# Query sketches on eight 32x64 PE tiles, squares over 2048 columns, first loads reordered, all engines replanned

## The chip, the cores and the metric

The kernel runs on one core of one Trainium2 chip. Its engines are PE (TensorE, matmuls; PEld is its weight load), DVE (VectorE), ACT (ScalarE), POOL (GpSimd) and SP (SyncE, which here only issues DMAs). The metric is device microseconds of one launch, as the median of several runs. Matmuls write PSUM, which has eight banks of 512 float32 per partition; a name such as L447 is line 447 of the kernel before.

## The reference, cut to what matters

```python
# q, k, v: (4 batches, 4 heads, 1088 tokens, 32); S1, S2: (8, 32), all float32
def phi(x):                                   # 32 -> 64 features
    a = einsum('rd,bhsd->bhsr', S1, x)
    b = einsum('rd,bhsd->bhsr', S2, x)
    return einsum('bhsi,bhsj->bhsij', a, b).reshape(..., 64)
q_p, k_p = phi(q), phi(k)
kv  = einsum('bhsf,bhsd->bhfd', k_p, v);  z = k_p.sum(axis=2)
num = einsum('bhsf,bhfd->bhsd', q_p, kv)
den = einsum('bhsf,bhf->bhs', q_p, z)[..., None] + 1e-06
x = (num / den)  as (4352 tokens, 128)        # heads side by side
h = x @ w_in;  g = maximum(h, 0) ** 2         # w_in: 128 x 2048
out = g @ w_out                               # w_out: 2048 x 128
```

## The kernel before, in words

There are two parts, interleaved on all engines: a linear attention, batch by batch (`attention(b, vt)`), and a feed-forward over blocks of tokens (`ffn`).

**Attention of one batch.** SP loads k, q and v (L297, L333, L340), with four heads times 32 rows of tokens on the 128 partitions, and 34 tokens of 32 numbers side by side. DVE transposes k and q in 32x32 blocks (`tk` L365, `tq` L434), so that heads times 32 dimensions are on the partitions. For k, PE multiplies 32-column slices with the block-diagonal sketch `SK` (`ksk` L379), ACT copies one half of the result (`ka` L387), DVE multiplies both halves to 64 features (`kp` L395), and PE accumulates `kv` and `z` over all tokens (`kv` L412) in the one PSUM bank `a`; two small copies bring it to `kvz` (`kve` L425).

**The query sketch** stands at L440 to L464. A batch's 1088 query columns are handled in three groups of 384, 384 and 320. For each of S1 and S2 (`x`), PE runs two matmuls of 64 rows by 128 columns, one for each pair of heads (`qr` L447); `SR` holds a sketch repeated so that the product has all 64 features of both heads. Each fp32 matmul shows as two records in the profile. S1's result lies in one two-bank PSUM buffer `hA`, S2's in another, `hB`. ACT copies `hA` to SBUF (`qa` L456), which frees `hA`, and DVE multiplies `hB` with that copy into `qp` (`qp` L460), which frees `hB`.

Then PE forms numerator and denominator (`num` L477, 24 matmuls of 128x32 for a group), DVE divides (`mx`, L487 to L489), PE transposes (`tx` L500) and ACT or DVE writes the token columns into `xT` (`xe` L506).

**Feed-forward.** Nine blocks of 384, 7x512 and 384 tokens; 2048 hidden columns make eight pairs of 128 for each block. For a pair, PE makes two matmuls into an `h` buffer (`m1` L527), ACT applies Relu to bf16 (`r` L536), DVE squares 128x1024 (`g` L543), and PE accumulates two matmuls into `o` (`m2` L550). At the end of a block DVE transposes `o` (`oe` L557) and SP stores it (`st` L566) in pieces of 32 output dimensions. Weights come through POOL's queue, cast to bf16 (L275, L279), behind a small POOL copy that waits for the second piece of the first k (`gate` L271).

**PSUM**: three `h` buffers of two banks each, one `o` bank and one `a` bank: all eight. `num`, `tx` and `ksk` take `a` or `h`; sketches and `m1` take only `h`.

**The order** is the work of a small planner in the file (`Graph.run`, L62). Each operation has a cost for each engine that may do it, its predecessors, the buffers it needs and a due time `pri`; among the operations that can start within a look-ahead (`LOOK`) of the earliest one, the one with the least `pri` goes first, and where two engines are possible the one that ends first, with a penalty (0.6 us for a Relu on DVE). The list it gives is the order in which each engine issues. At most eight DMAs of the hardware queues are under way by its rule at L95.

```python
181  NH, NA, NR, NB = 3, 1, 4, 2
539  o2 = add(f"r.{n}.{m}", {"ACT": act(W * N), "DVE": dve(W * N, fix=0.16) + (0.6,)}, ...
544  o3 = add(f"g.{n}.{m}", {"DVE": dve(W * N, 0.53e-3, 0.1)}, ...
```

Of the kernel before, what the change touches and what calls it, by code (L numbers as in the profile page):

```python
# [15 lines left out]
SEM = 0.07  # L16
LOOK = 0.12
DMA_FIRST = 1.05
DMA_LAST = 1.2

# [8 lines left out]
class Op:  # L29
    def __init__(self, name, alts, fn, deps, pri, alloc, uses, port, dma, after):  # L30
        self.name, self.alts, self.fn, self.pri = name, alts, fn, pri
        self.deps = [d for d in deps if d is not None]
        self.alloc, self.uses, self.port, self.dma = alloc, uses, port, dma
        self.after = [d for d in after if d is not None]
        self.look = LOOK
        self.start = self.end = self.eng = None


class Graph:
# [22 lines left out]
    def run(self):  # L62
        eng_free, port_free, pipe = {}, 0.0, 0.0
# [8 lines left out]
        while ready:  # L72
            cands = []
            for o in ready:
# [11 lines left out]
                for e, (busy, lat, *pen) in o.alts.items():  # L86
                    pen = pen[0] if pen else 0.0
# [5 lines left out]
                    if e in o.port:  # L93
                        t = max(t, port_free)
                    if o.dma is not None and e != "POOL" and len(lanes) >= 8:  # L95
                        t = max(t, lanes[-8])
# [16 lines left out]
            eng_free[e] = t + busy  # L113
            if e in o.port:
                port_free = t + busy
# [15 lines left out]
def act(n):  # L131
    return (0.833e-3 * n + 0.17, 0.833e-3 * n + 0.2)


def dve(n, rate=1.042e-3, fix=0.07):
    return (rate * n + fix, rate * n + fix + 0.04)
# [6 lines left out]
def pe(t):  # L143
    return (t, t + 0.2)


@with_exitstack
def kernel(
# [29 lines left out]
    def P(name, shape, dt=F32):  # L178
        return ps.tile(shape, dt, name=name, tag=name)

    NH, NA, NR, NB = 3, 1, 4, 2
    G = Graph({"h": NH, "o": 1, "a": NA, "r": NR, "g": NR, "osb": 3, "den": 3, "A": 2})
    tiles = {
        "h": [P(f"h{i}", [128, 1024]) for i in range(NH)],
        "o": [P("o0", [128, 512])],
        "a": [P(f"a{i}", [128, 512]) for i in range(NA)],
        "r": [T(f"r{i}", [128, 1024], BF16) for i in range(NR)],
        "g": [T(f"g{i}", [128, 1024], BF16) for i in range(NR)],
        "osb": [T(f"osb{i}", [128, 512]) for i in range(3)],
        "den": [(T(f"den{i}", [128, 12]), T(f"rec{i}", [128, 12]), T(f"xs{i}", [128, 3, 128], BF16)) for i in range(3)],  # L190
        "A": [T(f"A{i}", [128, 2, 384]) for i in range(2)],
    }

    def at(buf):
        return tiles[buf.slot[0]][buf.slot[1]]

# [6 lines left out]
    mk2 = T("mk2", [128, 2])  # L203
    SK = T("SK", [128, 2, H, R])
    SR = T("SR", [128, 2, 2, R, R])
# [8 lines left out]
    vtl = [T(f"vtl{i}", [32, H, 2, D]) for i in range(NB)]  # L214
# [3 lines left out]
    kvz = [T(f"kvz{i}", [128, 2, 2, D + 1]) for i in range(NB)]  # L218
    qp = [T(f"qp{i}", [128, 2, S]) for i in range(NB)]
# [3 lines left out]
    SU = [None, None]  # L223
    for x, src in ((0, S1), (1, S2)):
        def f(e, x=x, src=src):
            en = nc.sync if e == "SP" else nc.scalar
            en.dma_start(out=S_sb[x::2, :], in_=src[None, :, :].to_broadcast([8, R, D]))  # L227
        SU[x] = add(f"S{x}", {"SP" if x else "ACT": (0.4, 2.0)}, f, pri=-200, dma=0.05)
    o_mkz = add("mkz", {"DVE": dve(4)}, lambda e: nc.vector.memset(mk4, 0.0), pri=-100)

    def f_mk(e):
        for h in range(H):
            nc.vector.memset(mk4[32 * h : 32 * h + 32, h : h + 1], 1.0)
        nc.vector.tensor_tensor(out=mk2, in0=mk4[:, 0:2], in1=mk4[:, 2:4], op=ALU.add)
    o_mk = add("mk", {"DVE": (0.4, 0.45)}, f_mk, [o_mkz], pri=-100)
    o_ST = add("ST", {"DVE": dve(32)}, lambda e: nc.vector.transpose(ST, S_sb), SU, -98)
# [3 lines left out]
    for x in range(2):  # L240
        def f(e, x=x):
            s = STx[:, x]
            s = s[:, None, None, :] if x else s[:, None, :, None]
            nc.vector.tensor_tensor(
                out=SR[:, x], in0=s.to_broadcast([128, 2, R, R]),
                in1=mk2[:, :, None, None].to_broadcast([128, 2, R, R]), op=ALU.mult)
        o_SR.append(add(f"SR{x}", {"DVE": dve(128)}, f, [o_ST, o_mk], -96))

# [7 lines left out]
    for i in range(NB):  # L256
# [6 lines left out]
        iot, pattern=[[1, 128]], base=0, channel_multiplier=-1), pri=-101)  # L263
# [7 lines left out]
    o_gate = add("gate", {"POOL": (0.1, 0.15)}, lambda e: nc.gpsimd.tensor_copy(gate, kin[0][:, S - 1 : S]), [], -45)  # L271
    gated = [o_gate]
    for lo, hi in ((0, 1), (1, 2), (2, 4)):
        def f(e, lo=lo, hi=hi):
            nc.gpsimd.dma_start(out=w_in[:, 512 * lo : 512 * hi], in_=moe_w_in[:, 512 * lo : 512 * hi])  # L275
        o_win.append(add(f"w_in{lo}", {"POOL": (0.9, 3.0)}, f, [z_ops[1]] + gated, -40 + lo, dma=0.8 * (hi - lo)))
# [3 lines left out]
        o_wout.append(add(f"w_out{lo}", {"POOL": (1.0, 3.0)}, f, [z_ops[1]] + gated, -39.5 + lo, dma=0.9 * (hi - lo)))  # L280
# [5 lines left out]
    hist = {}  # L286

# [3 lines left out]
    def attention(b, vt):  # L291
        i = b % NB
        mine = lambda key, op: hist.setdefault((b, key), []).append(op)

        def ld(dst, src, c0, c1):
            def f(e):
                nc.sync.dma_start(  # L297
                    out=dst[:, D * c0 : D * c1],
                    in_=src[b].rearrange("h (t c) d -> (h t) (c d)", c=C)[:, D * c0 : D * c1])
            return f  # L300

        def tok(j, g):
            if j == 8:
# [6 lines left out]
        o_kh = [add(f"ldk{b}.{c0}", {"SP": (0.4, 3.4)}, ld(kin[i], k, c0, c1), prev(b, "tk"), vt(0) - 30 + c0 / 16,  # L310
                    dma=1.6 * (c1 - c0) / 34) for c0, c1 in KS]
        if b == 0:
            o_gate.deps.append(o_kh[1])
            hist["order"] = []
        after = [] if b == 0 else list(hist["order"])
        if b == 1:
            for o in o_kh:
                o.after += after
        o_q = []
        QS = ((0, 12), (12, 34)) if b == 0 else ((0, 34),)  # L320
        for c0, c1 in QS:
            o_q.append(add(f"ldq{b}.{c0}", {"SP": (0.4, 3.4)}, ld(qin[i], q, c0, c1), prev(b, "tq"),
# [307 lines left out]
```

## Time and profile before

| | us |
|---|---|
| median of 3 runs (132.45 to 136.91) | 133.09 |
| span of the profiled execution | 130.5 |
| PE busy, 1572 matmul records | 115.0 |
| DVE busy, 170 instructions | 96.6 |
| ACT busy, 108 instructions | 81.6 |
| POOL busy, 30 instructions | 11.1 |
| first matmul (`ksk`) starts | 5.59 |
| first `m1` starts | 22.55 |
| last matmul ends, last `oe` starts | 125.5 |

The profiled execution spans 130.5 us from its first instruction to its last, 2.6 us less than the median of the runs; sums below are made against the span, and the 2.6 us are added at the end. Busy time of an engine counts instructions that overlap once. The chain of work that ended last is followed back from the last instruction, at each step to what released it. All DMAs together moved 10.22 MB, nearly all of the input in the first 32 us.

### The profile page before, as it was taken

What the parts mean: (1) busy time and instruction counts of PE and PEld (TensorE: products, weight loads), DVE (VectorE), ACT (ScalarE), POOL (GpSimd) and SP (SyncE); (2) the same over time, 40 slices, a digit from 0 to 9 for tenths busy, and PEclk for the clock granted to TensorE, in tenths of its full rate; (3) what the DMA queues carried; (4) which work ended last, traced back from release to release, by engine and by line L of the source; (5) the groups of instructions that cost most, each with busy time, mean ns of one, the idle gap of its engine ahead of it and who ended that gap; (6) DMA issues with size and microseconds to landing.
All of it is one profiled execution on the core that took longest, in us unless ns stands there. A gap on an engine that the chain in (4) does not pass through costs nothing.

```text
span 130.5 us, 3742 instructions
## 1 busy us (share of the span) xinstructions
PE 115.0 (88%) x1572; PEld 62.2 (48%) x1572; DVE 96.6 (74%) x170; ACT 81.6 (63%) x108; POOL 11.1 (9%) x30
## 2 busy tenths in 40 slices
PE   0279599599999899999999999999999999999930
PEld 0256365353565455455445655556355544444500
DVE  2486367969969999969837888798268977878840
ACT  0065023377636749986525979885377699999910
POOL 4091000504250000000000000000000000000000
PEclk9999959999999999999999999999999999999996
DMA  1999999996700210220130001301300040031402
GB/s 21 296 135 242 328 254 260 254 225 223 159 3 0 51 17 0 40 45 0 28 58 0 5 0 28 57 0 25 60 0 5 0 80 5 3 65 18 78 16 50
DMA packets 24225, 10.22 MB, mean 78 GB/s; under 512 B 19472, under 2 KB 22928, under 8 KB 24208
## 3 DMA queue, kind: packets, MB, share of 16 engines
q1 hardware_dynamic: 22280, 8.57, 28.1%
q0 software_dynamic: 992, 1.05, 5.3%
q10 hardware_dynamic: 936, 0.37, 1.3%
q8 instruction: 12, 0.20, 0.6%
q14 instruction: 5, 0.04, 0.1%
HBM read 8.80 MB, written 2.23 MB: 85 GB/s over the span
## 4 chain that ended last, share of the span: by engine, by line
PE 70%; DMA 9%; DVE 7%; ACT 6%; issue 2%; ACTq 2%; DVEq 0%
PE o L550 21%; PE h L527 18%; PE h L447 14%; ACT r L536 6%; PE a L412 5%; DMA qin<-in_q_dram 5%; PE a L477 4%; DMA vin<-in_v_dram 4%; PE h L477 3%; DVE g L543 3%; PE a L379 2%; DVE osb L557 2%; PE h L500 1%; PE h L379 1%; ACTq L227 1%
## 5 line engine op out<-in xcount | busy, mean ns | idle before, releaser
L536 ACT ACTIVATE r<-h 128x1024 bf16<-128x1024 f32 (+1 forms) x72 | 65.6, 1026 | 19.7 <-PE h L527 19.5
L543 DVE TENSOR_TENSOR g<-r 128x1024 bf16<-128x1024 bf16 (+1 forms) x72 | 46.8, 662 | 11.3 <-ACT r L536 10.7
L550 PE MATMUL o<-g,w_out 128*128 128x512 bf16 (+1 forms) x144 | 40.9, 368 | 0.7 <-DVE g L543 0.4
L527 PE MATMUL h<-xT,w_in 128*128 128x512 bf16 (+1 forms) x144 | 40.1, 369 | 0.7 <-ACT r L536 0.4
L447 PE MATMUL h<-qT,SR 64*128 64x384 f32 (+1 forms) x96 | 22.3, 560 | 1.3 <-DVE qT L434 1.3
L527 PEld LDWEIGHTS <-w_in 128*128 128x128 bf16 x144 | 15.1, 114 | 15.7 <-issue 4.5
L550 PEld LDWEIGHTS <-w_out 128*128 128x128 bf16 x144 | 12.1, 97 | 15.8 <-issue 6.9
L460 DVE TENSOR_TENSOR qp<-h,A 128x768 f32<-128x768 f32 (+1 forms) x12 | 10.9, 907 | 5.7 <-PE h L447 5.1
L456 ACT COPY A<-h 128x768 f32<-128x768 f32 (+1 forms) x12 | 9.2, 763 | 7.5 <-PE h L447 7.5
L447 PEld LDWEIGHTS h<-qT,SR 64*128 64x128 f32 x96 | 8.3, 202 | 9.0 <-issue 4.3
L412 PEld LDWEIGHTS a<-vp,kp 128*64 128x64 f32 x288 | 9.3, 143 | 3.7 <-issue 3.7
L412 PE MATMUL a<-vp,kp 128*64 128x33 f32 x288 | 10.1, 228 | 0.0
L379 PE MATMUL a<-SK,kT 128*32 128x64 f32 x168 | 3.8, 239 | 5.6 <-DVE kT L365 5.6
L365 DVE STREAM_TRANSPOSE kT<-kin 128x1088 f32<-128x1088 f32 (+2 forms) x5 | 5.4, 1073 | 3.0 <-DMA kin<-in_k_dram 3.0
L434 DVE STREAM_TRANSPOSE qT<-qin 128x384 f32<-128x384 f32 (+1 forms) x8 | 5.9, 734 | 2.0 <-DMA qin<-in_q_dram 1.9
L557 DVE STREAM_TRANSPOSE osb<-o 128x512 f32<-128x512 f32 (+1 forms) x9 | 6.1, 682 | 1.0 <-PE o L550 0.8
L395 DVE TENSOR_TENSOR kp<-a,ka 128x1024 f32<-128x1024 f32 (+1 forms) x5 | 6.4, 1272 | 0.6 <-ACT ka L387 0.6
L477 PEld LDWEIGHTS h<-kvz,qp 128*32 128x32 f32 x288 | 5.0, 120 | 3.1 <-issue 1.5
L379 PEld LDWEIGHTS a<-SK,kT 128*32 128x32 f32 x168 | 2.9, 121 | 7.1 <-DVE kT L365 5.6
L350 POOL COPY vp<-vin 128x512 f32<-128x512 f32 x6 | 4.1, 706 | 22.9 <-DMA vin<-in_v_dram 16.2
L477 PE MATMUL h<-kvz,qp 128*32 128x66 f32 x288 | 6.1, 238 | 0.0
L477 PEld LDWEIGHTS a<-kvz,qp 128*32 128x32 f32 x288 | 4.4, 109 | 2.5 <-issue 1.3
(42 smaller groups left out, 55.0 us busy)
## 6 DMA issues: line engine op xcount, KB each, us to landing
kin<-in_k_dram SPq DMA_DIRECT2D x3, 544.0 KB, 8.4
qin<-in_q_dram SPq DMA_DIRECT2D x3, 544.0 KB, 8.2
vin<-in_v_dram SPq DMA_DIRECT2D x12, 128.0 KB, 8.3
out_dram<-osb SPq DMA_DIRECT2D x16, 64.0 KB, 1.9
out_dram<-osb SPq DMA_DIRECT2D x8, 48.0 KB, 2.2
qin<-in_q_dram SPq DMA_DIRECT2D x1, 352.0 KB, 6.6
vin<-in_v_dram ACTq DMA_DIRECT2D x5, 64.0 KB, 4.1
out_dram<-osb SPq DMA_DIRECT2D x8, 40.0 KB, 1.7
```

What stands on the lines that cost most here:

```text
L379: nc.tensor.matmul(o[32 * g : 32 * g + 32, :, j - j0, :], lt, SK.rearrange("p x h r -> p x (h r)"), start=True, stop=True)
L395: nc.vector.tensor_tensor(out=kp[i][:, j0:j1].rearrange("p j h (x y) -> p (j h) x y", y=R), in0=bb[:, :, None, :].to_broadcast([128, m, R, ...
L412: nc.tensor.matmul(t[64 * (h % 2) : 64 * (h % 2) + 64, 33 * (h // 2) : 33 * (h // 2) + 33], kp[i][:, j, h, :], vp[i][:, h, j, :], start=(j ...
L447: nc.tensor.matmul(at(hb)[:, 512 * pr : 512 * pr + n], SR[64 * pr : 64 * pr + 64, x].rearrange("p a x y -> p (a x y)"), qT[i][64 * pr : 64 ...
L456: nc.scalar.copy(at(sA)[:, :, 0:n], at(hA).rearrange("p (m s) -> p m s", m=2)[:, :, 0:n])
L460: nc.vector.tensor_tensor(out=qp[i][:, :, c0 : c0 + n], in0=at(hB).rearrange("p (m s) -> p m s", m=2)[:, :, 0:n], in1=at(sA)[:, :, 0:n], o ...
L477: nc.tensor.matmul(t[32 * cc : 32 * cc + 32, x, 2 * pr : 2 * pr + 2, :], qp[i][:, pr, 32 * c : 32 * c + 32], kvz[i][:, pr], start=True, st ...
L527: nc.tensor.matmul(at(hb)[:, step * w : step * w + N], w_in[:, 512 * (ct // E) : 512 * (ct // E) + 512].rearrange("p (c e) -> p e c", e=E) ...
L536: nc.scalar.activation(o, view(at(hb)), ACTF.Relu)
L543: nc.vector.tensor_tensor(out=at(gb)[:, 0 : W * N], in0=r, in1=r, op=ALU.mult)
L550: nc.tensor.matmul(at(ob)[:, 0:N], w_out[:, ct, :], at(gb)[:, N * w : N * w + N], start=(ct == 0), stop=(ct == CT - 1))
L557: nc.vector.transpose(at(sbuf)[:, 0:N], at(ob)[:, 0:N])
```

## The change

1. **Sketches.** q is loaded so that the first half of a group's token columns lies on partitions 0 to 63 and the second half on partitions 64 to 127 (the two classes of the title); the 64 partitions of a class are two heads times 32 rows of tokens, and the two other heads lie beside them in further columns. That makes six loads for a batch where there were one, or two for the first batch. A group is now 192, 192 or 160 columns in each of four sections. For a group, eight matmuls of 32 rows by 64 columns are issued for S1 and eight for S2, over four row groups and two column halves. Both results lie side by side in two `h` buffers (four banks), from column 0 and from column 256, and both buffers are held until `qp` is done. `SR` needs no mask. `kvz` and `qp` take four sections; `num` reads them with the same number of matmuls.
2. **PSUM** is one tile of eight banks with the same division; `tx` writes into the buffer of its own `num` in place of another one.
3. **Squares** take two pairs at once (2048 columns), with three `r` and three `g` buffers of that size; in the last block the last two pairs stay single. A square may also go to ACT.
4. **First loads.** Both sketches go through ACT's queue; a tiny ACT copy is put at the start; the gate waits for the first two pieces of q; v of the first batch is split over SP, ACT and POOL; the last two token rows of v go straight into `vp`, without a copy; loads of later batches wait until the first `w_out` load was issued. The first batch's k features and `kv` go in three parts, not two.
5. **Stores** of the last block alternate between SP and ACT.
6. **Plan.** The planner's constants change, it charges 0.11 us for a change of PE tiling, and a table of some 750 entries gives each operation its own due time, look-ahead and engine penalty.

```diff
-    NH, NA, NR, NB = 3, 1, 4, 2
+    NH, NR, NB = 3, 3, 2
+    ps = P("ps", [128, 4096])
...
+    def both(b0, b1, c0, n):
+        lo, hi = sorted((b0.slot[1], b1.slot[1]))
+        v = ps[:, 0:3072].rearrange("p (s u c) -> p s u c", s=3, c=512)
+        return v[:, lo : hi + 1 : hi - lo, :, c0 : c0 + n]
...
+    add("table", {"ACT": (1.45, 1.5)}, lambda e: nc.scalar.copy(warm[:, 0:1], warm[:, 1:2]), [o_mk], pri=-66)
...
-    o_gate = add("gate", {"POOL": (0.1, 0.15)}, lambda e: nc.gpsimd.tensor_copy(gate, kin[0][:, S - 1 : S]), [], -45)
+    o_gate = add("gate", {"POOL": (0.1, 0.15)}, lambda e: nc.gpsimd.tensor_copy(gate, qin[0][:, 383:384]), [], -45)
...
+        qsrc = q[b].rearrange("(p a) (t c) d -> (a t) p (c d)", a=2, c=C)
+        for j0, j1 in GJ:
+            for cls in range(2):
+                def f_q(e, j0=j0, j1=j1, cls=cls):
+                    w = 32 * (j1 - j0)
+                    c0 = 64 * j0 + cls * w
+                    nc.sync.dma_start(
+                        out=qin[i][64 * cls : 64 * cls + 64, 64 * j0 : 64 * j0 + 2 * w].rearrange(
+                            "x (p s) -> x p s", p=2),
+                        in_=qsrc[:, :, c0 : c0 + w])
...
+                qu = "SP" if b else "POOL" if a else "ACT" if g < 2 else "SP"
...
-            for x, hb in ((0, hA), (1, hB)):
-                def f_m(e, x=x, hb=hb, c0=c0, n=n):
-                    for pr in range(2):
-                        nc.tensor.matmul(
-                            at(hb)[:, 512 * pr : 512 * pr + n],
-                            SR[64 * pr : 64 * pr + 64, x].rearrange("p a x y -> p (a x y)"),
-                            qT[i][64 * pr : 64 * pr + 64, c0 : c0 + n], start=True, stop=True)
+            def f_m(e, h0=h0, h1=h1, j0=j0, n=n):
+                t = both(h0, h1, 0, 512)
+                for x in range(2):
+                    for p in range(2):
+                        for rg in range(4):
+                            cls, u = rg // 2, rg % 2 ^ p
+                            nc.tensor.matmul(
+                                t[64 * u : 64 * u + 64, cls, p, 256 * x : 256 * x + n],
+                                SR[32 * rg : 32 * rg + 32, x].rearrange("p x y -> p (x y)"),
+                                qT[i][32 * rg : 32 * rg + 32, 64 * j0 + p * n : 64 * j0 + p * n + n],
+                                start=True, stop=True)
...
+            def f_ac(e, h0=h0, h1=h1, sA=sA, n=n):
+                nc.scalar.copy(at(sA)[:, :, :, 0:n], both(h0, h1, 0, n))
...
+                    out=qp[i].rearrange("p (s u) c -> p s u c", s=2)[:, :, :, 32 * j0 : 32 * j0 + n],
+                    in0=both(h0, h1, 256, n), in1=at(sA)[:, :, :, 0:n], op=ALU.mult)
...
-            def f_g(e, rb=rb, gb=gb):
-                r = at(rb)[:, 0 : W * N]
-                nc.vector.tensor_tensor(out=at(gb)[:, 0 : W * N], in0=r, in1=r, op=ALU.mult)
+            def f_g(e, rb=rb, gb=gb, num=num):
+                r = at(rb)[:, 0 : W * N * num]
+                g = at(gb)[:, 0 : W * N * num]
+                if e == "ACT":
+                    nc.scalar.activation(g, r, ACTF.Square)
+                else:
+                    nc.vector.tensor_tensor(out=g, in0=r, in1=r, op=ALU.mult)
+            o3 = add(f"g.{n}.{first}", {"DVE": dve(W * N * num, 0.533e-3, 0.14), "ACT": act(W * N * num)}, f_g, o2,
...
+                q_st = "ACT" if n0 + N == N_TOK and db % 2 else "SP"
...
+        pairs = ((0, 2), (2, 2), (4, 2))
+        ffn(n, starts[n], N, starts[n] / 64.0, pairs + (((6, 1), (7, 1)) if n0 == starts[n] + N else ((6, 2),)))
+    for o in G.ops:
+        if o.name in plan:
+            o.pri, o.look, o.pen = map(float, plan[o.name])
```

## The prediction

> **What bounds the kernel now.** I read the time in three stretches first: the start (to 26.3 us), the middle (to 104) and the end.
>
> ```profile
> 0.00:26.30 26.30, 16.96 (x354) 11.23 (x355) 16.03 (x34) 7.65 (x16) 6.83 (x22) 0.94 0.93 224
> 26.30:104.00 77.70, 77.24 (x1122) 41.04 (x1122) 62.70 (x109) 53.60 (x69) 4.31 (x8) 1.00 0.20 43
> 104.00:130.50 26.50, 20.76 (x99) 9.89 (x96) 17.88 (x30) 20.36 (x25) 0.00 (x0) 0.96 0.22 39
> ```
>
> The columns are the stretch, its length, then busy time of PE, PEld, DVE, ACT and POOL, the granted clock, DMA share and GB/s. In the middle PE is busy 77.24 of 77.70 us, while DVE has 15.0 us and ACT 24.1 us to spare. A busy PE is not yet a bound, so the second view is the chain of waits of the page.
>
> ```profile
> PE 70%; DMA 9%; DVE 7%; ACT 6%; issue 2%; ACTq 2%; DVEq 0%
> PE o L550 21%; PE h L527 18%; PE h L447 14%; ACT r L536 6%; PE a L412 5%; DMA qin<-in_q_dram 5%; PE a L477 4%; DMA vin<-in_v_dram 4%; PE h L477 3%; DVE g L543 3%; PE a L379 2%; DVE osb L557 2%; PE h L500 1%; PE h L379 1%; ACTq L227 1%
> ```
>
> PE is 70% of it, and the query sketch (L447) 14%, 18 us: the largest piece after the feed-forward matmuls. The chain in order of time prices the pieces (start, length, what).
>
> ```profile
> 59.49 0.84 PE h L447 x4
> 60.34 1.06 PE a L412 x32
> 61.39 0.54 PE o L550 x2
> 61.93 0.84 PE h L447 x4
> 62.78 0.56 PE h L527 x2
> ...
> 67.94 0.74 PE h L447 x4
> 68.68 0.83 PE a L477 x48
> ```
>
> One sketch, one of S1 or S2 for one group, takes 0.84 us (384 columns) or 0.74 (320); a numerator group of 48 records 0.83. A feed-forward pair is 0.43 where it follows its like, and 0.54 to 0.56 behind or ahead of another tiling: some 0.11 us for a change. Last, the groups, for what ACT and DVE pay (line, shape, count, busy, mean ns).
>
> ```profile
> L536 ACT ACTIVATE r<-h 128x1024 bf16<-128x1024 f32 x56 | 53.9, 1055 | 16.3 <-PE h L527 16.0
> L543 DVE TENSOR_TENSOR g<-r 128x1024 bf16<-128x1024 bf16 x56 | 37.8, 685 | 10.1 <-ACT r L536 10.0
> ...
> L543 DVE TENSOR_TENSOR g<-r 128x768 bf16<-128x768 bf16 x16 | 9.0, 580 | 1.2 <-ACT r L536 0.7
> ```
>
> **Sketches.** Removed: per batch 4 x 0.84 + 2 x 0.74 = 4.84 us of PE, 19.4 in all. The price of the new form is not in the trace, so I bound it. From 384 to 320 columns a sketch falls by 0.10 us, 1.6 ns per column over two passes, so 384 columns stream in 0.62 us and 0.22 us is weight loading. With all eight tiles at once, 192 columns stream in 0.31 us for each of S1 and S2; with 0.1 us for the loads (half as wide) that is 0.82 for a group of 192 and 0.72 for one of 160, 2.36 us per batch. If the two column halves run one after the other, everything doubles: 4.7, no gain. If only half of the loading and issue overlaps, 3.0. The nearest row is the numerator: 48 records of 66 columns in 0.83 us is 17 ns a record, where 66 columns at 0.8 ns a pass are 53 ns, so at least three of its four column tiles do run together; and 64 records at 17 ns would be 1.1 us, which bounds the group if issue is the limit. I take 2.4 per batch, with 3.5 as the bad end of this. Saved: 4 x 2.44 = 9.8 us (5.4 at the bad end). In addition twelve blocks replace 24, so up to twelve changes of tiling at 0.11 go: 1 us.
>
> Here two rules of the Trainium skill speak against the change. "TensorE: Matmul & The Clock Gate", Part 3, says that a weight load overlaps a running matmul only where the row group differs; the second four matmuls of each S use the same four row groups, so by it a group would cost 1.6 us and this part would save nothing. The numerator's matmuls all take the same 128 rows, and their 17 ns a record contradicts the rule as far as column tiles go. "TensorEngine Tiling (Array Packing)", Restrictions and Gotchas, says that different row tiles cannot access one PSUM bank at the same time, and here two row groups write two halves of one bank; the kernel before never does that, so no row decides it, and if it serialized them the group would again be near 1.6 us. The sum would then be 11 us higher.
>
> **What the sketches cost elsewhere.** ACT copies and DVE products keep their size (4 x 192 = 768 columns; rows 799 and 950 ns), and ACT no longer has S1 alone to start on: it waits 0.4 us longer. Both buffers are now held from the first matmul to the end of `qp`: 0.8 + 0.05 + 0.80 + 0.05 + 0.95 = 2.65 us each, 5.3 buffer-us a group. Before, 59.42 to 61.18 and 61.86 to 63.89 made 3.8. Against that `tx` needs no buffer of its own.
>
> **Squares.** Two rows give 105 ns for 256 columns, 0.41 ns a column, so 265 ns of a square is fixed; in pairs without idle time they follow at 0.64, so less of it may be real. 35 mergers save 0 to 9 us of DVE, I take 5. None of it is on the path in the middle, where PE ends last; it is what lets DVE keep up. The price is that an `m2` waits for a second Relu (1.06 us). Six pairs fit into the `r` buffers instead of four, and `m1` and attention cover it; without that cover it is 1 us per merger. A square on ACT would be 2048 columns at the Relus' (1055 - 923)/256 = 0.52 to 1 ns, 1.2 to 2.1 us, a work that ACT's idle 24 us holds for about ten. The profile has one table load (L387, 1.28 us) and none between Copy and Relu; whether Square needs another no row shows: 2.6 us a square if so, so I keep that in the bad cases.
>
> **The start.** PE idles 9.3 us there: 5.6 before the first `ksk`, 3.7 later. The path to the first `m1`:
>
> ```profile
> 11.42 2.67 PE L412 MATMUL a<-vp,kp 128*64 128x33 f32 x72
> ...
> 15.31 0.18 DVE L425 COPY kvz<-a 64x66 f32<-64x66 f32 x1
> ...
> 16.80 1.55 PE L477 MATMUL h<-kvz,qp 128*32 128x66 f32 x48
> ```
>
> `kv` ends at 14.1, the small copies stand behind a q transpose of 0.91 us until 15.3, and the numerator behind a sketch until 16.8; `m1` comes at 22.55, behind two more sketches and a `ksk`. By rows alone (0.4 copies, 0.9 numerator, 1.0 division, 0.35 transposes, 0.5 copy, 0.3 waits) it could come 3.5 us after `kv`, at 17.6. The first w_in piece lands at 6.65 + 5.7 = 12.4, so it doesn't hold this, but the last two land at 20 and 22, so pairs 4 to 7 cannot run before. S1's issue on SP (0.78 us) no longer precedes k: 0.8 us earlier; S1 then queues behind S0's 1.21 us on ACT, covered because `SK` is due only when k's transpose ends at 5.5, else 0.5 lost. The early table load saves up to 1.28 us ahead of the first `ka`. Four v loads at 0.6 us each stand on POOL's queue, inside its 4.1 us of waiting for the gate; if they fall behind it, the weights are 2.4 later. Five extra q issues of 0.43 us per batch lie on SP, whose later loads are needed 10 us after landing; the same bytes in shorter runs may slow DMA, and in the start its share is 0.93. In idle time I take 1.5 us of gain (bounds -2 and +5), plus 1.1 us from half as much sketching at the low clock: the sketch's records took 7.03 us there, against 4.84 at full clock.
>
> **The middle turns from one bound to nearly three.** PE falls by 7.3 (three batches) + 0.8. DVE's 62.7 less 24 mergers (3.4) is 59.3 and ACT's stays 53.6, in about 70 us: 85% and 77%. The 0.5 us of PE idle will not stay at 0.5; I take 4 (2 to 9).
>
> **The end.** ACT's Relus run without a gap from 104.86 to 124.4, 0.914 us a pair where PE would take 0.86; some Relus on DVE save at most 1 us. Two of four last store issues (0.45 us each) on ACT save 0.8. I take 1.3 together, less 0.3 for the late wait of merged squares.
>
> **Sum.** 130.5 - 9.8 - 1.0 (changes) - 1.5 - 1.1 (start) + 3.5 (new idle in the middle) - 1.0 (end) = 119.6 us of span; with the 2.6 between span and median, 122.2.
>
> **The rivals.** (a) *ACT and DVE become the bound.* For it: 85% and 77% on average, with stretches where DVE was full already (5.00 of 5 us from 30 to 35); against it, its work is 18 us less than the span. Then idle in the middle is 9, the start gives nothing: 122.2 + 5.5 + 1.5 = 129. (b) *The new tiling doesn't run side by side.* Sketches cost 4.7 per batch as now, 9.8 + 1 return, ACT and DVE have room again (-2): 131, no change. For it, no 32x64 tile in the trace; against it, the numerator's 17 ns. (c) *PSUM starves the feed-forward: slower.* While a group holds two `h` buffers for 2.65 us, pairs have one `h`, and each needs it for 0.43 + 1.05 + 0.1 = 1.6 us against 0.86 of PE. With 1.8 us left after the matmuls that loses 0.8 us a group, 7 in the middle, if nothing else is ready, and only offsets the gain. It decides for slower when each hold grows by about 1.3 us, one Relu and a part of a square queued ahead of the copy and the product: 12 x 2.1 = 25 us lost, less the half that numerators, `kv` and waiting `m2` fill: 122.2 + 15 = 137. Against it: per batch the holds (17 pairs x 1.6, groups 16, numerators 8, k features 5, `kv` 6) are 62 of 4 x 25 buffer-us.
>
> **How the numbers follow.** Forecast 0.65 (117 to 126), (a) 0.16, (b) 0.09, (c) 0.10. What this kernel's measurement can tell from no change is 2%: below 130.4 is faster, above 135.8 slower. Faster: 0.65 + 0.12 of (a) + 0.03 of (b) = 0.80; same: 0.04 + 0.06 = 0.10; slower: 0.10. The range from 116.5 to 130.5 leaves out (c), half of (b) and a little at the bottom, where the start gives its 5 us and the middle stays full.
>
> **What would show it.** Right: a group's 32 sketch records span about 0.8 us; PE idles 2 to 9 us in its middle; the first `m1` starts between 17 and 21. Wrong: 1.6 us for a group (b); table loads between Square and Relu; DVE above 95% there with PE waiting on `g` (a); `m1` waiting on ACT's copy or DVE's product with both engines idle elsewhere (c).

## The result and the profile after

The changed kernel takes 126.31 us (median of 4 runs, 125.34 to 129.84), the kernel before beside it 133.38 us (132.45 to 136.91): a ratio of 0.9525, 95% interval 0.9372 to 0.9678. The time lies inside the forecast's range, 4.1 us above its sum of 122.2. Some executions take a few per cent longer whatever the kernel, so the ratios here leave these out while medians are over all runs, and the profile shown as "after" is that of a second execution of the same kernel (span 124.2 us), in place of the first, slower one (127.7).

Three stretches, cut at the start of the second feed-forward pair (28.00 us here, 25.61 before) and at the beginning of the end. First the kernel before, then the changed one; the columns are as in the prediction (stretch, length, busy PE, PEld, DVE, ACT, POOL, clock, DMA share, GB/s).

```profile
0.00:25.61 25.61, 16.47 (x352) 11.00 (x353) 15.34 (x33) 7.16 (x14) 6.83 (x22) 0.93 0.93 225
25.61:104.00 78.39, 77.73 (x1127) 41.27 (x1125) 63.39 (x110) 54.09 (x70) 4.31 (x8) 1.00 0.21 44
104.00:130.50 26.50, 20.76 (x99) 9.89 (x96) 17.88 (x30) 20.36 (x25) 0.00 (x0) 0.96 0.22 39
```

```profile
0.00:28.00 28.00, 17.07 (x461) 13.52 (x462) 13.40 (x30) 7.48 (x16) 8.60 (x24) 1.00 0.87 200
28.00:105.00 77.00, 75.07 (x1334) 43.36 (x1328) 64.65 (x90) 66.69 (x78) 3.34 (x4) 1.00 0.23 49
105.00:124.20 19.20, 14.50 (x74) 7.37 (x71) 13.56 (x15) 13.67 (x16) 0.00 (x0) 0.99 0.25 43
```

From the second pair to the last instruction the kernel before needs 130.5 - 25.6 = 104.9 us, the changed one 96.2: 8.7 us gained. In the start 2.4 us are lost. The 8.7 are 8.9 us less PE work (77.73 + 20.76 against 75.07 + 14.50), 1.3 us more idle time in the middle (0.66, now 1.93) and 1.0 less at the end (5.74, now 4.70). The cut is not quite fair: ahead of its second pair the changed kernel has 40 more `ksk` records (0.77 us) and three transposes fewer (0.33), so 0.4 us of the PE work only stands on the other side of the cut. PE is still the bound in the middle, with 75.07 of 77.00 us, although ACT is now busy for 66.69 of them.

The page's chain of waits and, from the same chain in order of time, the rows of a sketch (L599) and a numerator (L631):

```profile
PE 60%; DVE 13%; DMA 7%; SPq 6%; ACT 6%; issue 5%; DVEq 0%; ACTq 0%
PE ps L681 17%; PE ps L713 16%; PE ps L555 8%; PE ps L631 8%; PE ps L599 8%; DVE g L703 5%; ACT r L691 4%; DMA qin<-in_q_dram 3%; DMA kin<-in_k_dram 3%; DVE r L693 2%; DVE qp L613 2%; SPq L459 2%; PE ps L655 2%; SPq L475 2%; DVE osb L720 2%
```

```profile
61.58 0.84 PE ps L599 x32
62.42 0.54 PE ps L713 x2
...
65.66 0.73 PE ps L599 x32
66.39 0.83 PE ps L631 x48
```

One row of L599 is now S1 and S2 together: 0.84 us for 192 columns and 0.73 for 160, where each of the two took 0.84 or 0.74 alone. PE's share of the chain fell from 70 to 60%, the sketch's from 14 to 8%. The groups give what ACT and DVE pay now (Relu, square on DVE, square on ACT, copy of the sketch):

```profile
L691 ACT ACTIVATE r<-ps 128x1024 bf16<-128x1024 f32 x51 | 49.4, 1029 | 7.4 <-PE ps L681 5.6 <-DVE den L642 0.8 <-DVE xs L644 0.3
...
L703 DVE TENSOR_TENSOR g<-r 128x2048 bf16<-128x2048 bf16 x24 | 29.1, 1226 | 5.5 <-ACT r L691 5.1
...
L701 ACT ACTIVATE g<-r 128x2048 bf16<-128x2048 bf16 x4 | 7.7, 1918 | 0.1
...
L609 ACT COPY A<-ps 128x768 f32<-128x768 f32 x8 | 6.4, 797 | 7.7 <-PE ps L599 7.3
```

Last the start, on PE's timeline: start, length, then in brackets the idle time before it and what ended it.

```profile
9.72 1.92 PE L555 MATMUL ps<-vp,kp 128*64 128x33 f32 x32 [1.19 <-DVE kp L535]
11.57 1.58 PE L599 MATMUL ps<-qT,SR 32*64 32x192 f32 x32
13.09 2.35 PE L555 MATMUL ps<-vp,kp 128*64 128x33 f32 x40
16.07 1.55 PE L631 MATMUL ps<-kvz,qp 128*32 128x66 f32 x48 [0.64 <-issue]
17.55 1.58 PE L599 MATMUL ps<-qT,SR 32*64 32x192 f32 x32
20.09 0.48 PE L655 MATMUL ps<-ident,xs 128*128 128x128 bf16 x3 [0.96 <-ACT A L609]
21.14 0.80 PE L681 MATMUL ps<-xT,w_in 128*128 128x384 bf16 x2 [0.57 <-ACT xT L661]
...
28.00 0.52 PE L681 MATMUL ps<-xT,w_in 128*128 128x384 bf16 x2
```

Two things are to be seen. Every row up to 24 us takes almost twice what it takes later: a sketch 1.58 where the middle has 0.84, a `kv` part of 32 records 1.92 where it has 1.06. This looks like a low clock, although the table's column of the granted clock reads 1.00 there; the last section comes back to that. And the transposes of L655 wait for ACT's copy of a sketch (L609), which has nothing to do with them.

### The profile page after: what moved, and what is told of

Same layout as the page of the kernel before. It is cut to its first block, busy times and chain, and to the rows that moved or that the text cites. A ratio compares the mean times of both kernels' runs of the same rounds, so it can differ in the third digit from the quotient of the medians.

```text
span 127.7 us, 4266 instructions
## 1 busy us (share of the span) xinstructions
PE 104.3 (82%) x1841; PEld 63.3 (50%) x1860; DVE 91.7 (72%) x132; ACT 88.1 (69%) x109; POOL 10.9 (9%) x28
## 4 chain that ended last, share of the span: by engine, by line
PE 56%; DVE 14%; DMA 10%; issue 6%; ACT 6%; SPq 5%; ACTq 1%; DVEq 0%
PE ps L681 16%; PE ps L713 15%; PE ps L631 8%; PE ps L555 7%; PE ps L599 6%; DMA kin<-in_k_dram 5%; DVE g L703 4%; ACT r L691 4%; DMA qin<-in_q_dram 2%; SPq L459 2%; DVE r L693 2%; DMA S_sb<-in_S_dram 2%; DVE qp L613 2%; PE ps L655 2%; DVE osb L720 2%
## 5 line engine op out<-in xcount | busy, mean ns | idle before, releaser
L691 ACT ACTIVATE r<-ps 128x1024 bf16<-128x1024 f32 (+1 forms) x64 | 59.5, 985 | 16.1 <-PE ps L681 5.9
L681 PE MATMUL ps<-xT,w_in 128*128 128x512 bf16 (+1 forms) x133 | 38.3, 372 | 5.7 <-DVE qp L613 3.2
L713 PE MATMUL ps<-g,w_out 128*128 128x512 bf16 (+1 forms) x136 | 38.2, 369 | 1.4 <-issue 0.5
L703 DVE TENSOR_TENSOR g<-r 128x2048 bf16<-128x2048 bf16 (+2 forms) x29 | 33.3, 1161 | 7.2 <-ACT r L691 6.5
L613 DVE TENSOR_TENSOR qp<-ps,A 128x768 f32<-128x768 f32 (+1 forms) x12 | 10.9, 907 | 8.7 <-ACT A L609 7.5
L609 ACT COPY A<-ps 128x768 f32<-128x768 f32 (+1 forms) x12 | 9.1, 762 | 9.3 <-PE ps L599 4.1
L631 PE MATMUL ps<-kvz,qp 128*32 128x66 f32 x576 | 12.1, 234 | 2.7 <-DVE qp L613 1.2
L631 PEld LDWEIGHTS ps<-kvz,qp 128*32 128x32 f32 x576 | 9.9, 117 | 6.9 <-issue 3.6
L701 ACT ACTIVATE g<-r 128x2048 bf16<-128x2048 bf16 (+2 forms) x8 | 13.0, 1621 | 0.1
L599 PE MATMUL ps<-qT,SR 32*64 32x192 f32 (+1 forms) x384 | 11.8, 356 | 0.4
L535 DVE TENSOR_TENSOR kp<-ps,ka 128x1024 f32<-128x1024 f32 (+3 forms) x9 | 10.7, 1210 | 1.7 <-ACT ka L527 1.7
L555 PE MATMUL ps<-vp,kp 128*64 128x33 f32 x288 | 10.8, 233 | 1.2 <-DVE kp L535 1.2
L599 PEld LDWEIGHTS ps<-qT,SR 32*64 32x64 f32 x384 | 7.2, 144 | 3.8 <-issue 1.4
```

The lines of the kernel that those rows point to most:

```text
L535: nc.vector.tensor_tensor(out=kp[i][:, j0:j1].rearrange("p j h (x y) -> p (j h) x y", y=R), in0=bb[:, :, None, :].to_broadcast([128, m, R, ...
L555: nc.tensor.matmul(t[64 * u : 64 * u + 64, 33 * (h // 2) : 33 * (h // 2) + 33], kp[i][:, j, h, :], vp[i][:, h, j, :], start=(j == 0 and h ...
L599: nc.tensor.matmul(t[64 * u : 64 * u + 64, cls, p, 256 * x : 256 * x + n], SR[32 * rg : 32 * rg + 32, x].rearrange("p x y -> p (x y)"), qT ...
L613: nc.vector.tensor_tensor(out=qp[i].rearrange("p (s u) c -> p s u c", s=2)[:, :, :, 32 * j0 : 32 * j0 + n], in0=both(h0, h1, 256, n), in1= ...
L631: nc.tensor.matmul(t[32 * cc : 32 * cc + 32, x, 2 * pr : 2 * pr + 2, :], qp[i][:, 2 * cls + pr, 32 * j : 32 * j + 32], kvz[i][:, 2 * pr : ...
L681: nc.tensor.matmul(at(hb)[:, 512 * w : 512 * w + N], w_in[:, 512 * (ct // E) : 512 * (ct // E) + 512].rearrange("p (c e) -> p e c", e=E)[: ...
```

## The experiments

All ran beside the kernel before. The changed kernel itself, with nothing edited:

> The changed kernel again, unaltered, as the base for the others. Both theories expect 125 to 126 us, a sketch group at 0.80 to 0.84 us of PE, the first m1 near 20.4 us and DVE waiting about 3.4 us for the last batch's k near 42 us; if that last wait is absent here, it belonged to the one profiled execution and not to the kernel.

It took 126.32 us (125.03 to 127.61), ratio 0.957 (0.943 to 0.971), and gave the profile above. The wait of 3.4 us near 42 us is 0.6 there, so it belonged to the first profiled execution and not to the kernel.

### What the gain consists of

**Each sketch computed twice.** This puts most of the removed PE work back, in the new tiling, without touching anything else.

```diff
-                for x in range(2):
+                for x in (0, 1, 0, 1):
```

> Every sketch group is computed twice into the same place, so that PE pays 1.6 us a group, what the old tiling paid, and all else stays. Theory (PE ends last, so its saving arrives in full): 12 groups x 0.8 = 9.6 us longer, with the low clock in the first groups 10 to 12, so 135 to 138 us: without the sketches' gain the change would be a loss. Rival (PE, ACT and DVE bound together, so part of PE's saving was only turned into idle time): 4 to 7 us longer.

132.57 us (131.87 to 135.84, 10 runs), ratio 1.005 (0.999 to 1.010). These are the sketches (L599) behind the second pair, in the changed kernel and in this one, and then all work of this one:

```profile
28.00:105.00 77.00, 7.91 (x288) 4.94 (x288) 1.00 0.23 49
...
28.63:105.00 76.37, 13.51 (x576) 10.54 (x576) 1.00 0.22 47
...
28.63:105.00 76.37, 75.03 (x1591) 46.12 (x1587) 59.70 (x84) 61.53 (x72) 2.35 (x4) 1.00 0.22 47
105.00:129.80 24.80, 20.11 (x103) 10.16 (x100) 18.85 (x21) 19.27 (x22) 0.00 (x0) 1.00 0.23 40
```

PE got 5.6 us more work there, and the time from the second pair on grew from 96.2 to 101.2 us. So 5.0 of 5.6 us (89%) arrive. (The expected 9.6 us took 0.8 for each group; the second computation costs 0.6.) PE's idle time did not grow (6.0 us, 6.6 in the changed kernel), although the doubled sketches hold their buffers longer: it is the work that costs. In the kernel before, the sketches behind the second pair took 15.30 us; with most of that put back, nothing of the gain is left.

**The plan's table taken out.** Everything else of the change stays, and the order comes from the planner's constants alone.

```diff
-        if o.name in plan:
+        if False and o.name in plan:
```

> The changed kernel without its table of due times, look-aheads and penalties, so ordered by the planner's own constants alone; everything else of the change stays. If the table is what keeps the three engines full in the middle (the idle time that was forecast at 4 us and came out at some 1.3), PE idles 5 us or more there and the time is 130 to 134, most of the gain gone. If the tiling and mergers carry the gain by themselves: 126 to 128.

131.43 us (129.89 to 132.84, 4 runs) beside 132.55 (131.45 to 135.48), without an interval. In its profile the second pair starts at about 27.3 us, but from there on it needs 101 us, and the middle shows why; below it are PE's waits in it (who waits for whom, us in total, times, the longest).

```profile
30.00:105.00 75.00, 67.99 (x1250) 39.38 (x1266) 56.83 (x76) 58.07 (x76) 2.43 (x4) 1.00 0.22 45
...
PE ps L681 <- DVE qp L613: 2.8, 3, 1.6
PE ps L599 <- DVE qp L613: 1.2, 2, 0.7
PE ps L681 <- ACT A L609: 1.2, 2, 0.6
```

PE idles for 7.0 of 75 us, against 1.2 in the changed kernel (73.80 of the same 75), and 5.2 of the 7.0 end with a sketch's product or copy, which hold the `h` buffers. DVE and ACT are busy for 57 and 58 us, less than in the changed kernel. The sketches freed 9 us of PE; the table is what lets PE use it. Either alone gives little: that is the second half of the explanation. No run gives the old tiling a table made for it, so what a table is worth by itself stays open.

**Squares in single pairs.** The merged square is issued as two instructions in the same place.

```diff
-                r = at(rb)[:, 0 : W * N * num]
-                g = at(gb)[:, 0 : W * N * num]
+                for u in range(num):
+                    r = at(rb)[:, W * N * u : W * N * (u + 1)]
+                    g = at(gb)[:, W * N * u : W * N * (u + 1)]
...
```

> Each merged square is made as two instructions of half the columns at the same place in the order; m2 still waits for both. DVE pays 24 x (2 x 0.685 - 1.22) and 4 x (2 x 0.58 - 0.96) more, about 4.4 us, ACT about 7 x 0.17 = 1.2 us. Theory (DVE has 15% to spare from 30 us on and PE ends last): at most 1 us longer. Rival (DVE shares the bound): 2 to 4 us longer.

126.40 us (126.01 to 126.64), ratio 0.957 (0.951 to 0.963): no difference in the time. Two singles at 681 ns follow each other closely enough that DVE's busy time rises by only 1.2 us (92.8 against 91.6) over 28 more instructions. In its profile the part from the second pair on takes 97.2 us, 1.0 more than in the changed kernel's, behind a start that was 0.8 us shorter; so the merging as such is worth 1 us at most. The buffers, and the plan made around them, stayed.

```profile
L704 DVE TENSOR_TENSOR g<-r 128x1024 bf16<-128x1024 bf16 x48 | 30.6, 681 | 2.4 <-ACT r L691 2.4
```

### What the start lost

**S1's load on SP**, behind the first piece of k, as before the change (there it was ahead of k). S landed at 5.0 us after the change and at 3.1 before.

```diff
-            nc.scalar.dma_start(out=S_sb[x::2, :], in_=...)
+            (nc.sync if x else nc.scalar).dma_start(out=S_sb[x::2, :], in_=...)
...
+    order.remove(names["S1"])
+    order.insert(order.index(names["ldk0.0"]) + 1, names["S1"])
```

> Only the issue of S1 moves back to SP, behind the first k load. Theory (the sketch matrices land 1.8 us later than before and hold the first k transpose behind them on DVE): S lands near 3.5 us in place of 4.9, the first ksk starts 1 to 1.5 us earlier, and 0.5 to 1.4 us of it reaches the end. Rival (the start waits for the second pieces of k and q): the first ksk starts earlier and the time stays within 0.3 us, or rises by up to 0.8 as q is issued later.

127.61 us (127.38 to 127.82), ratio 0.970 (0.966 to 0.974): slower by 1.3 us. S still landed at 5.0, and k's second piece came later, so PE waits in the middle of `ksk`:

```profile
6.36 1.08 PE L518 MATMUL ps<-SK,kT 128*32 128x64 f32 x32 [6.36 <-DVE kT L503]
9.14 1.30 PE L518 MATMUL ps<-SK,kT 128*32 128x64 f32 x40 [1.70 <-DVE kT L503]
```

The second pair starts 1.2 us later, at 29.17, and the end is later by 1.4. The edit did not cure what it was made for; what it lost in the start, it lost at the end too.

**PE kept warm.** Twenty bf16 matmuls of 512 columns on a constant, whose result nobody reads, stand in PE's early gaps.

```diff
+            for _ in range({"mk": 10, "ksk0.2": 3, "kv0.2": 2, "qr0.1": 3, "tx0.0": 2}.get(o.name, 0)):
+                nc.tensor.matmul(tiles["o"][0][:, 0:512], wk[:, 0:128], wk, start=True, stop=True)
...
```

> Added work, whose results nobody reads: 20 bf16 matmuls of 128x128x512 on PE, ten ahead of the first ksk and the rest in gaps of PE's first 21 us. In the changed kernel the same pieces take twice as long until about 24 us as after it (32 records of kv 1.92 against 1.06 us, a sketch group 1.58 against 0.84, a numerator group 1.55 against 0.83, two m1 matmuls 0.80 against 0.49). Theory (PE's clock stays low until 24 us, because the new start keeps PE less busy than the old one did, where kv and the later sketches ran at full speed from 11.4 and from 18.3 us): with the filler these pieces take their later durations from 6.4 us on, the first m1 starts 2 to 4.5 us earlier and the time falls by 2 to 4 us. Rival (loads, weights and DVE set the start, the low clock is hidden): durations halve, but the time stays within 0.7 us. A third: the filler does not change the durations, and the slowness is not a matter of PE's business.

127.78 us (125.38 to 130.35), ratio 0.954 (0.944 to 0.963): the same as the changed kernel. Yet the rows did become short from 6.5 us on:

```profile
10.01 1.13 PE L557 MATMUL ps<-vp,kp 128*64 128x33 f32 x32 [1.02 <-ACT ka L529]
11.07 0.91 PE L601 MATMUL ps<-qT,SR 32*64 32x192 f32 x32
...
14.02 0.66 PE L633 MATMUL ps<-kvz,qp 128*32 128x66 f32 x31 [0.22 <-DVE qp L615]
16.25 0.48 PE L633 MATMUL ps<-kvz,qp 128*32 128x66 f32 x17 [1.57 <-issue]
...
22.73 0.89 PE L633 MATMUL ps<-kvz,qp 128*32 128x66 f32 x43 [0.35 <-issue]
...
26.73 0.31 PE L633 MATMUL ps<-kvz,qp 128*32 128x66 f32 x3 [0.53 <-issue]
```

The second pair comes at 26.97, only 1.0 us earlier. Much of the gain went into something else: in the middle of a group of equal matmuls PE stands still, 1.57 + 0.35 + 0.53 us, with nothing that the profile shows to wait for. More on these pauses at the end. (This execution, with a span of 128.2 us, also has the late load of k at 45 us that is described below.)

**No waits on the buffer between.** Sketches hold two of three `h` buffers, read by one strided view (`both`). Where the two are not neighbours, the framework that inserts the semaphores takes the view to cover the buffer between them too, and makes its users wait. That concerns the first batch, whose three groups all got buffers 0 and 2; the wait of 0.96 us of the transposes, in the rows above, is one of these. A first edit only changes places, so that 0 and 2 lie side by side.

```diff
+    POS = (0, 2, 1)
...
-        "h": [ps[:, 1024 * i : 1024 * i + 1024] for i in range(NH)],
+        "h": [ps[:, 1024 * i : 1024 * i + 1024] for i in POS],
...
```

> Only the place of the three h buffers in PSUM is permuted, so that the first batch's sketches take two neighbouring buffers; order and work stay. Theory (waits on whole stretches of banks): in the changed kernel tx, the ACT copies, qp and the first Relu of the first batch each wait for work in the buffer that lies between the two of a sketch; by its rows tx lost 0.9, qp of group 1 lost 1.2, the first Relu 1.0 and the last ACT copy 1.2 us, partly on top of each other. Then tx of the first group follows the division without a copy between, the first m1 comes 0.9 to 1.5 us earlier and the time falls by 1 to 2.5 us. Rival (loads, weights and the low clock set the start): the waits move, the time stays within 0.5 us.

126.30 us (125.89 to 127.18), ratio 0.962 (0.949 to 0.974). The transposes no longer wait:

```profile
19.49 0.50 PE L656 MATMUL ps<-ident,xs 128*128 128x128 bf16 x3
```

The second pair came at 26.56, 1.4 us earlier than in the profile above; but four profiles with one and the same start (the two of the changed kernel, single squares, k early) have it between 27.16 and 28.20, so only 0.6 us of it are clear of that spread. Two groups of later batches now lie apart, and from the second pair on 97.6 us are needed, 1.4 more. The second edit also issues the copy and the product as two instructions wherever the buffers are not neighbours, so that no such wait is left:

```diff
-                nc.scalar.copy(at(sA)[:, :, :, 0:n], both(h0, h1, 0, n))
+                v = both(h0, h1, 0, n)
+                for c in near(h0, h1):
+                    nc.scalar.copy(at(sA)[:, c, :, 0:n], v[:, c])
...
```

> As the permuted buffers, but in the two sketch groups whose two buffers are still not neighbours the ACT copy and the DVE product are made as two instructions, one for each buffer, so that no wait for a third buffer is left anywhere; this costs about 0.2 us of ACT and 0.15 us of DVE, twice. Theory (the 1.4 us that the permutation gained at 28 us was given back by the same kind of wait between 60 and 70 us, where PE had 0.8 us of new idle time, and in 40 to 50 us): PE is full again there and the time falls by 0.8 to 1.5 us against the changed kernel. Rival (what is gained in the start is lost to ACT and DVE later in any case): within 0.4 us of it.

126.74 us (125.05 to 129.14), ratio 0.949 (0.940 to 0.958), span 123.4: a little less, not separated from the changed kernel by its interval.

**The last batch's k earlier** on SP, ahead of that batch's last q piece. In the changed kernel's first profile (127.7 us) that k landed at 45.3, and DVE, whose next instruction was its transpose, stood for 3.4 us; in the profile shown above it is 0.6.

```diff
+    order.remove(at_name["ldk3.0"])
+    order.insert(order.index(at_name["ldq3.6.1"]), at_name["ldk3.0"])
```

> Only SP's order is changed: the last batch's k load goes ahead of that batch's q loads instead of behind most of them. Theory (one early k transpose blocks DVE, behind it qp, so h buffers, m1 and ACT): DVE's wait of 3.4 us at 42 us is gone, PE's hole of 3.2 us with it, the time falls by 2 to 3.4 us. Rival (ACT and DVE are the bound in the middle, a hole is made up later): less than 1 us.

126.21 us (126.06 to 126.45), ratio 0.960 (0.956 to 0.964): no gain over an execution that has no such hole to close.

**Together.** All three edits, and the two without the warming matmuls:

> The changed kernel with three edits at once: 20 early warming matmuls, no wait on a buffer that lies between two others, and the last batch's k loaded before that batch's last q piece. If the lost start is low clock plus added waits and these are the whole of it, their gains add: dense feed-forward by 27.0 (29.4 in the changed kernel) and a span of 122, time 124. If PE's pauses with nothing to wait for (the instruction stream under full DMA) are a cause of their own, the added matmuls bring more of them: dense feed-forward at 28 to 29, time 125 to 126, no better than the changed kernel's undisturbed runs.

> The same without the 20 warming matmuls: no waits on the buffer between, and the last batch's k loaded earlier, which should close the 3 us hole of the disturbed executions. If the added waits cost what the chain showed in the start (some 1 us): 125.0 to 125.5 and no run above 127. If they only moved idle time: 126.2 as the changed kernel.

With warming 127.10 us (125.68 to 131.50), ratio 0.951 (0.944 to 0.958): no better, with pauses of 2.31, 0.23 and 1.57 us. Without it 124.47 us (122.93 to 124.94), ratio 0.938 (0.931 to 0.944). That last interval lies below those of the runs with k early alone and with single squares, so the kernel was run once more:

> The kernel of the run without added waits and with the last batch's k early, once more, beside new runs of the kernel before. If its gain over the changed kernel is the program's: a ratio of 0.93 to 0.945 again, 123 to 125 us, dense feed-forward before 29. If that run's chip or moment gave it: 0.95 to 0.96, as the changed kernel has had in every run.

123.51 us (122.83 to 125.09), ratio 0.939 (0.928 to 0.951), span 120.7. The twelve runs of this kernel, on two chips, lie at 125.09 us or below, and the eight of the changed kernel at 125.03 or above; the changed kernel did not run beside the second six. Its start, cut again at the second pair, and rows of it (L640 numerator, L604 sketch, L664 transposes, L690 feed-forward):

```profile
0.00:24.95 24.95, 13.63 (x461) 11.11 (x461) 13.43 (x30) 7.48 (x16) 8.61 (x24) 1.00 0.83 187
```

```profile
15.92 1.13 PE L640 MATMUL ps<-kvz,qp 128*32 128x66 f32 x48 [0.64 <-ACT kvz L576]
16.98 0.91 PE L604 MATMUL ps<-qT,SR 32*64 32x192 f32 x32
18.17 0.34 PE L664 MATMUL ps<-ident,xs 128*128 128x128 bf16 x3 [0.28 <-DVE xs L653]
19.22 0.48 PE L690 MATMUL ps<-xT,w_in 128*128 128x384 bf16 x2 [0.71 <-ACT xT L670]
...
20.96 0.59 PE L640 MATMUL ps<-kvz,qp 128*32 128x66 f32 x25
23.21 0.49 PE L640 MATMUL ps<-kvz,qp 128*32 128x66 f32 x20 [1.67 <-issue]
```

The same 461 records precede the second pair. They take 13.63 us of PE instead of 17.07, and the idle time is the same (11.32 against 10.93): the transposes now wait for their own operand (0.28 us) and the first feed-forward pair comes 1.9 us earlier, but a pause of 1.67 takes the place of the waits. What remains is 3.4 us of PE time on the same records. That the two edits together gain some 2 us is shown by the times. That they do so through the clock is not shown: the 461 records took 15.0, 15.1, 16.9 and 17.1 us in the four profiles with the unchanged start, and 15.0 in the other profile of this kernel (span 122.8), where they slowed once more behind a pause of 1.94 us. So 2.0 of the 3.4 us lie within what one start varies by, and where the gain of 2 us comes from stays open.

## Why the prediction was right, and which step failed

The likeliest case happened, for its own reason; the failed step is the start. It came out 7.6 us worse than its two terms, and the time stayed near the sum in part by luck, since PE work and idle time behind the start came out 3.0 us better.

| term of the sum, us | forecast | measured |
|---|---|---|
| PE work from the second pair on (sketches 7.3, tiling 0.8) | -8.1 | -8.9 |
| idle time in the middle | +3.5 | +1.3 |
| the end | -1.0 | -1.0 |
| start, PE work (sketches 2.4, tiling 0.2, low clock 1.1) | -3.7 | +0.6 |
| start, idle time | -1.5 | +1.8 |
| span | 119.6 | 124.2 |

The terms are rounded. Measured values are differences of the two tables of stretches above; 16.47 and 17.07 us of PE work and 9.14 and 10.93 of idle time stand for the start. The 0.4 us of PE work on the other side of the cut make the first row larger and the fourth worse.

**Sketches: right.** Taken were 0.82 and 0.72 us for a group, measured 0.84 and 0.73. The forecast's bound of 1.1 us by issue counted 64 records in a group; there are 32. Behind the second pair the sketches fell from 15.30 to 7.91 us, 7.4 where 7.3 were forecast. The two rules weighed against the change did not show. The forecast took "TensorE: Matmul & The Clock Gate", Part 3 (a weight load overlaps a running matmul only where the row group differs) and "TensorEngine Tiling (Array Packing)", Restrictions and Gotchas (different row tiles cannot access one PSUM bank at the same time) to mean near 1.6 us for a group; measured are 0.84, and 1.58 only in the start, where all rows take nearly twice as long. So rival (b) fell, and the run with doubled sketches shows that this saving carries the gain.

**Squares: right in kind, too large in size.** The merger was to save 5 us of DVE; undone, it costs 1.2 of DVE and at most 1 us of time. The bad case of a table load between Relu and Square fell: a Square of 2048 columns on ACT takes 1.92 us, inside the 1.2 to 2.1 given, with 0.1 us of idle time in all before four of them.

**The middle: too pessimistic.** 3.5 us of new idle time (1.5 to 8.5 by the range) came out at 1.3. Rivals (a) and (c) lay in this term, and the run without the table shows that (c) was real: there PE idles 7.0 us, 5.2 of them until a sketch's copy or product, with ACT and DVE free for 17 and 18 of 75 us. The forecast judged the buffers and engines by averages and had no price for the plan, which is what keeps those waits away.

**The end: right in size.** No run separates its parts, the Relus on DVE and the stores on two queues.

**The start: wrong in sign.** "In idle time I take 1.5 us of gain (bounds -2 and +5), plus 1.1 us from half as much sketching at the low clock" was the step. The idle time came out near the bad bound, 1.8 us more. Two causes were seen: S lands 1.9 us later (the first `ksk` at 6.38 instead of 5.59; the forecast held this covered, or 0.5 us lost), and the transposes wait 0.96 us for work on the buffer between. PE's pauses are no cause here: the profile of the kernel before has one of 1.55 us, that of the changed kernel none (last section). And the PE work of the start did not fall. Its sketches did, from 7.03 to 4.54 us. But in the kernel before, `kv` (72 records in 2.67 us) already ran at nearly full speed at 11.4 us; after the change its two parts, in slow rows, took 4.27, and `ksk`, with the 40 records more, 4.00 instead of 3.03. The forecast took the low clock as given and let it only shrink with the sketches; the profiles show that the time at which rows become short moves by many microseconds, between executions of one kernel too. The mark chosen for the start was a poor one as well: the first pair came at 21.14, just outside the forecast's 17 to 21, and 6.9 us of attention follow before the second, where it was 3.1 before.

## What to carry to other kernels

Price a removed matmul by the nearest tiled rows of the trace, then ask what lets its engine use the freed time: here the tiling without the plan (131.4 us beside 132.6), and the plan with most of the old sketching (132.6 beside 132.5), each brought little or nothing. Split a start's forecast into work, idle time and clock, and measure it at the point from which the bound engine runs without gaps, not at the first instruction of the main loop. A strided view over buffers that are not neighbours can tie what lies between into its waits; look for waits between operations that share no data.

## What the runs showed of the hardware

**The clock comes up at different times.** Where the profile records a granted clock of half, the rows take twice as long. In the kernel before, these stretches hold a numerator group of 1.55 us (16.80) and one of 0.90 (21.72); the granted clock is the third number from the end:

```profile
16.80:18.30 1.50, 1.50 (x52) 1.32 (x50) 1.21 (x1) 0.80 (x1) 0.00 (x0) 0.50 1.13 249
21.72:22.55 0.83, 0.83 (x50) 0.74 (x49) 0.64 (x1) 0.00 (x0) 0.00 (x0) 1.00 1.09 276
```

In the changed kernel's profile the column reads 1.00 over the whole start, but the trace holds no clock record there: the first one, at full clock, begins at 24.8 us, and the column counts what is ahead of it as full. So the low clock of its start is read from its rows, which are as long as those at 0.50. In the first profile of the same kernel the same rows became short at about 15 us (46 numerator records in 0.90 us at 15.73; slow once more from 20.9 to 24), in this one only at 24. "TensorE: Matmul & The Clock Gate", Part 1, has the clock rise after about 3.4 us of sustained work and calls the moment variable between runs; here `kv` and a sketch ran without a gap from 9.72 to 15.4 us, and the sketch at 17.55 still took 1.58, so that the figure does not hold in this profile. Twenty bf16 matmuls from the beginning on brought the short rows by 6.5 us.

**PE can pause at steps of 128 matmul records in the first 28 us.** In kernels with different numbers of early matmuls the pauses stand behind the same count of records. With 20 extra matmuls they come after records 222, 350 and 478 (the rows of 31, 5 and 45 records that each end there); with doubled sketches, in another line, after 350 and 478:

```profile
21.66 0.58 PE L518 MATMUL ps<-SK,kT 128*32 128x64 f32 x25
23.62 0.32 PE L518 MATMUL ps<-SK,kT 128*32 128x64 f32 x7 [1.38 <-issue]
...
25.88 0.33 PE L518 MATMUL ps<-SK,kT 128*32 128x64 f32 x9
27.35 0.65 PE L518 MATMUL ps<-SK,kT 128*32 128x64 f32 x31 [1.14 <-issue]
```

and without either, after 350 (72 + 32 + 32 + 40 + 48 + 32 + 3 + 2 + 32 + 32 + 25 records to the pause of 1.67 us shown above). The kernel before has one too, behind 349 records:

```profile
23.84 0.10 PEld L500 LDWEIGHTS <-xs 128*128 128x128 bf16 x1
25.45 0.33 PE L500 MATMUL h<-ident,xs 128*128 128x128 bf16 x3 [1.55 <-DVE rec L488]
```

The profile puts it down to DVE's `rec`, but that had ended at 23.2; the operand `xs` was ready at 23.8, the weight load followed at once, and its matmul came 1.6 us later. So the pauses did not come with the change. With one weight load for each record, 128 records are 256 instructions. The page's table of queues has a queue of its own for instructions:

```profile
q8 instruction: 14, 0.23, 0.8%
```

14 packets of 0.23 MB together are 16 KB each, 64 bytes for each of 256 instructions. The trace has the time of every packet, and with it the pauses come out as waits for instructions. Ten profiles hold 17 pauses of more than 0.2 us; each ends 1.3 to 1.7 us after a packet has landed, the first packet for record 222, the second for 350, the third for 478 (21.86 and 23.21 us for the pause of 1.67 us). In no profile does PE pass one of these places sooner after its packet. So rows that become short early bring PE there ahead of its instructions: with the 20 extra matmuls it reached record 222 at 14.7 us, and the packet landed at 14.85.

Why a packet is late is less sure. The pauses were seen only up to 28 us, where the DMA share is 0.8 to 0.9 on average, not in the middle, where it is 0.2. The packet behind record 222 begins 2.5 to 4.2 us after PE has passed that record, the one behind record 606, at 33 to 44 us, 2.3 us after at most. That the packets queue behind the loads would fit this, but it was only argued: no run took the loads away. The sizes differ from execution to execution, from nothing to 2.3 us.
